# Row maxima of an attention: one standing scratch tile for their discarded scores, and another place for the scores in the second stretch

## The chip, the cores and the metric

The kernel runs on one core of a Trainium2 chip. The metric is the device time of one execution in microseconds (us); less is better. The core's engines are named as in the profile: PE multiplies matrices (PEld is its loading of weights), DVE is the vector engine, ACT the engine that evaluates functions, POOL the general one, SP an engine that here only issues DMAs. Each engine runs its own list of instructions in order and waits on semaphores that the others count up.

## The reference

Four layers act on x of 2048 rows by 640 columns, each as `x = x + layer(layernorm(x))`, in the order A, B, A, B. A is a linear attention. B has 32 heads of 20 columns and cuts the 2048 rows into four segments of 512; within a segment it is a causal softmax attention, and a memory carries what earlier segments left.

```
for s in range(N):                      # N = 4 segments of L = 512 rows
    qs, ks, vs = q[:, :, s], k[:, :, s], v[:, :, s]
    logits = jnp.einsum("bhqd,bhkd->bhqk", qs, ks) * scale + mask
    p = _softmax(logits, axis=-1)
    a_dot = jnp.einsum("bhqk,bhkd->bhqd", p, vs)
    pq = phi(qs)
    num = jnp.einsum("bhld,bhde->bhle", pq, M)
    den = jnp.einsum("bhld,bhd->bhl", pq, z)[..., None] + 1e-6
    a_mem = num / den
    o = g * a_mem + (1.0 - g) * a_dot
    outs.append(o)
    pk = phi(ks)
    M = M + jnp.einsum("bhld,bhle->bhde", pk, vs)
    z = z + jnp.einsum("bhld->bhd", pk)
```

## The kernel before

Two streams of work are written into one program. `dense` holds the layer norms, the projections, the memories and the outputs; `attend` holds the softmax of the two B layers. `run` takes a piece of the one or of the other by their costs so far, so PE's list is a hand-made mixture of both, and it stands as written (`MANUAL = ("PE",)`). The lists of DVE, ACT, POOL and SP are put in order by the framework's scheduler.

The attention goes by iterations, 8 groups of four heads for each of 4 segments and two B layers: 64 iterations in all, each of three stretches (`STRETCHES`, L54). Between two stretches PE gets a share of the dense stream. An entry of a stretch is an operation, its number, and how many groups back the group lies on which it works:

- `max` (`row_max`, L988) makes scores with queries on the partitions (L999), two banks a time, and lets DVE take each row's maximum over the masked keys (L1006). DVE's instruction must write the masked scores somewhere; nobody reads them. They go to a tile named `junk`. One `max` makes two or four such pieces: numbers 0 and 2 (with this table's numbering, `MAXES[0]` and `MAXES[2]`) two pieces of 512 columns, 1 and 3 a piece of 384 and one of 128 for each bank, 4 two of 256 for each. A piece is two DVE instructions: the reduction, and a short one that reads the accumulator out into `mg`.
- `split` (L1010) turns the maxima into two 16-bit rows `m2` on DVE (L1015, L1016); `rows` (L1019) transposes them on PE (L1024), copies them on ACT (`mt`, L1026) and sends them with two DMAs of SP's queue (L1029) into the query tile `qs` of the group.
- `exp` (`scores`, L1032) makes scores with keys on the partitions, the row maxima already taken off by the rows that `rows` has put into `qs` (L1041: two banks for each `exp`), then ACT takes the exponential (L1045) and POOL the causal mask (L1052).
- `sum` (L1060, L1068) weighs the values, `copy` (L1072) empties that bank, `out` (`normalize`, L1076) transposes back (L1081) and divides (L1084, L1091).

So in the second stretch of an iteration the new group gets its fourth maximum, and the group before it, whose rows were sent in the first stretch, its first scores.

PSUM has 8 banks, handed out in turn to both streams (`bank`, L144): the bank that PE fills now must have been read out by the engine that used it 8 banks ago. The tile `junk` comes from a pool with one buffer (`bufs=1`): each piece asks for the tile anew, and it is released when the piece before has been read out.

Of the kernel before, what the change touches and what calls it, by code (L numbers as in the profile page):

```python
# [11 lines left out]
BF16 = mybir.dt.bfloat16  # L12
# [9 lines left out]
P = 128  # L22
C = D // P
SEG = 512
# [29 lines left out]

STRETCHES = [[("exp", 4, 2), ("max", 0, 0), ("max", 1, 0), ("sum", 0, 2), ("rows", 0, 1), ("sum", 1, 2), ("sum", 3, 2),
              ("sum", 2, 2), ("copy", 0, 2), ("max", 2, 0)],
             [("out", 0, 2), ("max", 3, 0), ("exp", 0, 1), ("exp", 1, 1)],
             [("exp", 2, 1), ("exp", 3, 1), ("max", 4, 0), ("split", 0, 0), ("load", 0, 0)]]


# [70 lines left out]
class Kernel:  # L131
# [702 lines left out]
    def open_b(self):  # L834
        self.bp = self.ctx.enter_context(self.tc.tile_pool(name="attn", bufs=1))
        nc = self.nc
        self.ks = [self.bp.tile([P, 2, SEG], F16, name=f"ks{j}") for j in range(3)]
        one = self.bp.tile([P, 2, SEG], F16, tag="nat", name="one", bufs=2)
        nc.vector.memset(one[:2], M_ONE)
        for k in self.ks:  # L840
            for a in (60, 124):
                nc.sync.dma_start(k[a:a + 2], one[:2])
# [147 lines left out]
    def row_max(self, G, todo):  # L990

        nc, bp, qs, ks = self.nc, self.bp, G["qs"], G["ks"]
        bs = [self.bank() for _ in range(2)]
        cost = 0
        for p, i, a in todo:
            n = (i + 1) * P
            for par in range(2):
                r = slice(64 * par, 64 * par + 60)
                nc.tensor.matmul(bs[par][:, a:a + n], qs[r, p, i * P:(i + 1) * P], ks[r, p, :n],  # L999
                                 start=True, stop=True)  # L1000
                cost += n * COL
        for par in range(2):
            for p, i, a in todo:
                n = (i + 1) * P
                junk = bp.tile([P, SEG], BF16, tag="junk", name="junk", bufs=1)
                nc.vector.tensor_tensor_reduce(junk[:, :n], bs[par][:, a:a + n], self.maskw[:, SEG - n:],  # L1006
                                               1.0, NEG, OP.add, OP.max, G["mg"][:, par, p, i:i + 1])
        return cost

# [318 lines left out]
```

## Time and profile before

| what | us |
|---|---|
| median of 3 runs (1766.63 to 1768.07) | 1767.3 |
| span of the profiled execution, first to last instruction | 1765.2 |
| PE busy in it | 1677.6 |
| DVE busy | 1190.2 |
| ACT busy | 969.2 |
| POOL busy | 519.6 |
| PE idle in the two B layers' attention (349 to 950, and 1238 to 1733) | 24.3 and 26.4 |

The median is 2.1 us above the span of the profiled execution. Busy is the time in which an engine has an instruction in work. PE's instructions overlap, and the profile models their ends, so a wait of PE that is shorter than the end of the matmul before it is not seen as idle time. A row of the waits says who waited, for whose instruction, how long in total, how often, and the longest.

### The profile page before, as it was taken

Reading aid. Unit: us, or ns where it says so; the run is one execution under the profiler, and the core shown is the slowest. Engines: PE = TensorE matmul, PEld = TensorE weight load, DVE = VectorE, ACT = ScalarE, POOL = GpSimd, SP = SyncE. Lnnn points to the kernel's source line nnn. Section 1 sums busy time; section 2 is a strip of 40 time slices with the busy share of each in tenths; the row PEclk is TensorE's granted clock in tenths of the full one; section 3 lists DMA queues with packets and bytes.
Section 4 is the critical chain, followed back from the end, with each engine's and each line's share of the span. In section 5 each row is a group of like instructions: output and inputs, shape, how many; then the busy total and the mean of one; then the engine's idle time right before and its main releaser. Section 6 shows DMA issues by size and latency. Waiting matters only on the chain.

```text
span 1765.2 us, 36353 instructions
## 1 busy us (share of the span) xinstructions
PE 1677.6 (95%) x13032; PEld 1046.0 (59%) x13032; DVE 1190.2 (67%) x3856; ACT 969.2 (55%) x1818; POOL 519.6 (29%) x982
## 2 busy tenths in 40 slices
PE   5989999999999999999989999999999999999998
PEld 4666667564565566456556777566446545644555
DVE  8554444487787777758865466746877877878773
ACT  5454443347656645666666453333665575666664
POOL 1533441012123412333342211221422432233442
PEclk9999999999999999999999999999999999999999
DMA  7432343422322332352211303433232323323422
GB/s 247 154 133 105 142 168 110 154 71 71 109 86 67 106 99 80 115 180 77 81 42 39 113 31 120 158 113 120 67 98 84 110 80 106 96 81 106 145 95 91
DMA packets 118333, 187.61 MB, mean 106 GB/s; under 512 B 13948, under 2 KB 79612, under 8 KB 115848
## 3 DMA queue, kind: packets, MB, share of 16 engines
q1 hardware_dynamic: 105896, 142.68, 25.5%
q0 software_dynamic: 3040, 21.63, 3.4%
q10 hardware_dynamic: 9216, 20.98, 3.1%
q8 instruction: 103, 1.69, 0.4%
q14 instruction: 78, 0.64, 0.1%
HBM read 106.05 MB, written 78.64 MB: 105 GB/s over the span
## 4 chain that ended last, share of the span: by engine, by line
PE 69%; DVE 13%; ACT 7%; issue 3%; DMA 3%; POOL 3%; SPq 1%; ACTq 0%; DVEq 0%; POOLq 0%
PE ps L388 30%; PE ps L374 15%; PE ps L1068 6%; DVE junk L1006 5%; ACT pe L1045 3%; PE ps L313 3%; PE ps L1041 3%; PE ps L999 3%; PE ps L557 3%; PE ps L443 2%; DMA pqi<-pqd 1%; PE ps L1081 1%; PE ps L884 1%; PE ps L723 1%; DVE st L331 1%
## 5 line engine op out<-in xcount | busy, mean ns | idle before, releaser
L1006 DVE CUSTOM_DVE_ANT_0 junk<-ps,maskw 128x512 bf16<-128x512 f32 (+3 forms) x1024 | 499.1, 487 | 91.3 <-PE ps L999 31.7
L1045 ACT ACTIVATE pe<-ps,lsc 128x512 f32<-128x512 f32 x640 | 394.6, 696 | 105.0 <-PE ps L1041 96.1
L1052 POOL TENSOR_SCALAR_AFFINE_SELECT pe<-pe 128x256 f32<-128x256 f32 (+1 forms) x640 | 231.3, 367 | 446.6 <-ACT pe L1045 442.4
L388 PEld LDWEIGHTS <-xT 128*128 128x128 f16 x2880 | 281.0, 98 | 115.6 <-issue 10.6
L388 PEld LDWEIGHTS <-oT 128*128 128x128 f16 x1920 | 185.9, 98 | 82.5 <-issue 7.5
L1068 PE MATMUL ps<-pe,v 128*32 128x512 f32 (+3 forms) x2048 | 161.1, 436 | 9.2 <-POOL pe L1052 4.2
L388 PE MATMUL ps<-w_Bo,oT 128*128 128x320 f16 x960 | 142.4, 301 | 2.3 <-ACT oT L317 1.2
L374 PE MATMUL ps<-xT,w_Bq 128*128 128x512 f16 x600 | 140.2, 379 | 1.9 <-ACT pe L1045 0.6
L374 PE MATMUL ps<-xT,w_Bk 128*128 128x512 f16 x600 | 138.8, 379 | 1.9 <-DVE tmp L1091 1.1
L388 PE MATMUL ps<-w_Bv,xT 128*128 128x320 f16 x960 | 139.7, 299 | 0.5 <-ACT v L421 0.5
L388 PE MATMUL ps<-w_Ak,xT 128*128 128x320 f16 x960 | 137.2, 300 | 0.6 <-ACT r L402 0.5
L999 PE MATMUL ps<-ks,qs 60*128 60x512 f16 (+3 forms) x1024 | 123.4, 299 | 10.2 <-DVE mg L1006 3.6
L1041 PE MATMUL ps<-qs,ks 62*128 62x384 f16 (+3 forms) x1024 | 112.7, 298 | 8.9 <-DVE mg L1006 5.7
L849 DVE SCALAR_TENSOR_TENSOR nat<-ps,nat 128x512 f16<-128x512 f32 x80 | 54.9, 686 | 83.8 <-ACT nat L848 78.3
L414 POOL TENSOR_SCALAR e<-e 128x320 f32<-128x320 f32 (+1 forms) x52 | 82.1, 1578 | 88.5 <-ACT e L410 85.5
L1068 PEld LDWEIGHTS ps<-pe,v 128*32 128x32 f32 x2048 | 63.4, 109 | 67.6 <-issue 43.0
L374 PEld LDWEIGHTS <-w_Bk 128*128 128x128 f16 x600 | 57.3, 98 | 71.6 <-issue 10.5
L848 ACT ACTIVATE nat<-ps 128x512 f16<-128x512 f32 x80 | 48.2, 602 | 92.5 <-PE ps L374 71.7
L374 PEld LDWEIGHTS <-w_Bq 128*128 128x128 f16 x600 | 56.8, 98 | 66.9 <-issue 8.9
L421 ACT ACTIVATE v<-ps 128x320 f32<-128x320 f32 x96 | 41.8, 437 | 90.3 <-PE ps L388 89.8
L336 POOL TENSOR_TENSOR rs<-rs,mhalf 128x1 f32<-128x1 f32 x48 | 27.0, 564 | 216.6 <-DVE rs L335 203.6
L466 POOL TENSOR_TENSOR xn<-xn,xo 128x320 f32<-128x320 f32 x56 | 48.7, 871 | 136.3 <-ACT xn L465 135.6
(220 smaller groups left out, 2680.2 us busy)
## 6 DMA issues: line engine op xcount, KB each, us to landing
x<-xn ACTq DMA_DIRECT2D x48, 320.0 KB
qs<-qd SPq DMA_DIRECT2D x128, 120.0 KB
ks<-kd SPq DMA_DIRECT2D x128, 120.0 KB
xo<-x SPq DMA_DIRECT2D x48, 320.0 KB
pqi<-pqd SPq DMA_DIRECT2D x32, 320.0 KB
qd<-nat SPq DMA_DIRECT2D x40, 256.0 KB
kd<-nat SPq DMA_DIRECT2D x40, 256.0 KB
x<-in_A_x SPq DMA_DIRECT2D x16, 320.0 KB
```

The costliest lines, as they stand in the source:

```text
L313: nc.tensor.transpose(pt[:, (c - c0) * P:(c - c0 + 1) * P], src[:, c * P:(c + 1) * P], self.ident)
L374: nc.tensor.matmul(p, w[:, c, a, t * P:(t + 1) * P], xT[:, c, b, :], start=k == 0, stop=k == 3 * C - 1)
L388: nc.tensor.matmul(p, xT[:, c, a, i * P:(i + 1) * P], w[:, c, b, n * HN:(n + 1) * HN], start=k == 0, stop=k == 3 * C - 1)
L414: nc.gpsimd.tensor_scalar(e, e, 1.0, eps, op0=OP.min, op1=OP.add)
L557: nc.tensor.matmul(p, xs[:, i, a, c * P:(c + 1) * P], pk[i][:, b, cols], start=k == 0, stop=k == 3 * NT - 1)
L849: nc.vector.scalar_tensor_tensor(nat[:, 1], p, QK_SHIFT, nat[:, 0], op0=OP.mult, op1=OP.subtract)
L999: nc.tensor.matmul(bs[par][:, a:a + n], qs[r, p, i * P:(i + 1) * P], ks[r, p, :n], start=True, stop=True)
L1006: nc.vector.tensor_tensor_reduce(junk[:, :n], bs[par][:, a:a + n], self.maskw[:, SEG - n:], 1.0, NEG, OP.add, OP.max, G["mg"][:, par, p, i ...
L1041: nc.tensor.matmul(b[:, a:a + n], ks[r, p, j * P:(j + 1) * P], qs[r, p, j * P:], start=True, stop=True)
L1045: nc.scalar.activation(e, b, AF.Exp, scale=self.lsc)
L1052: nc.gpsimd.affine_select(d, d, pattern=pat, compare_op=OP.is_ge, fill=0.0, base=0, channel_multiplier=-1)
L1068: nc.tensor.matmul(G["pv"][32 * h4:32 * h4 + 32, j * P:], v[j][:, h * E1:h * E1 + 32], G.pop((p, par, j)), start=j == 0, stop=j == 2, skip ...
```

## The change

The scratch tile becomes one that stands for the whole program, made once in `open_b`, and a piece writes to the columns in which its scores stand in their bank (`a:a + n`), no longer to the first columns (`:n`) of a tile of its own. So a piece of 384 columns and one of 128 no longer write over each other, nor do the two pieces of 256 of a bank. In the second stretch the two `exp` now come ahead of `max` 3. What is computed is the same.

```diff
-             [("out", 0, 2), ("max", 3, 0), ("exp", 0, 1), ("exp", 1, 1)],
+             [("out", 0, 2), ("exp", 0, 1), ("exp", 1, 1), ("max", 3, 0)],
...
         self.ks = [self.bp.tile([P, 2, SEG], F16, name=f"ks{j}") for j in range(3)]
+        self.junk = self.bp.tile([P, SEG], BF16, name="junk")
...
                 n = (i + 1) * P
-                junk = bp.tile([P, SEG], BF16, tag="junk", name="junk", bufs=1)
-                nc.vector.tensor_tensor_reduce(junk[:, :n], bs[par][:, a:a + n], self.maskw[:, SEG - n:],
+                nc.vector.tensor_tensor_reduce(self.junk[:, a:a + n], bs[par][:, a:a + n], self.maskw[:, SEG - n:],
                                                1.0, NEG, OP.add, OP.max, G["mg"][:, par, p, i:i + 1])
```

The lines from 838 to 1004 of the kernel before stand one line later in the changed one, so L999 is L1000 there; L1006 and what follows keep their numbers.

DVE's list at the second stretch of iteration 20, before (names carry buffer numbers; the row ends with the engines on whose semaphores it waits, DVE itself among them):

```order
L1084 RECIPROCAL rc4_9227<-ps_9222 128x16 [waits PE_49]
L1091 TENSOR_TENSOR tmp_9229<-ps_9222,rc4_9227 128x320 [waits DVE_49]
L1006 ISA junk_9238,mg_9109<-ps_9232,maskw_77 128x384 [waits PE_49]
L1006 ISA mg_9109 128x1
L346 BN_STATS st_9790<-xn_9112 128x6 [waits Pool_49]
L1006 ISA junk_9240,mg_9109<-ps_9232,maskw_77 128x128 [waits DVE_49]
L1006 ISA mg_9109 128x1
L1006 ISA junk_9242,mg_9109<-ps_9233,maskw_77 128x384 [waits DVE_49,PE_49]
L1006 ISA mg_9109 128x1
L1006 ISA junk_9244,mg_9109<-ps_9233,maskw_77 128x128 [waits DVE_49]
L1006 ISA mg_9109 128x1
```

The same place in the changed kernel:

```order
L1084 RECIPROCAL rc4_8900<-ps_8895 128x16 [waits PE_49]
L1091 TENSOR_TENSOR tmp_8902<-ps_8895,rc4_8900 128x320 [waits DVE_49]
L346 BN_STATS st_9423<-xn_8793 128x6 [waits Pool_49]
L1006 ISA junk_2761,mg_8790<-ps_8925,maskw_77 128x384 [waits PE_49]
L1006 ISA mg_8790 128x1
L1006 ISA junk_2761,mg_8790<-ps_8925,maskw_77 128x128
L1006 ISA mg_8790 128x1
L1006 ISA junk_2761,mg_8790<-ps_8926,maskw_77 128x384 [waits DVE_49,PE_49]
L1006 ISA mg_8790 128x1
L1006 ISA junk_2761,mg_8790<-ps_8926,maskw_77 128x128 [waits DVE_49]
L1006 ISA mg_8790 128x1
```

The four pieces of the maximum now stand together, the other stream's L346 is ahead of them; the first piece of 128 waits for nothing, and the two waits on DVE that are left are for the piece two places back that wrote the same columns, not for the one directly ahead.

PE's list at the same stretch, before (L1081 is `out`, L999 the fourth maximum, L1041 the scores; the weights are loaded by the row above each matmul):

```order
L1081 MATMUL ps_9222<-ident_68,oTf_9194 128x128 x3
L999 LDWEIGHTS qs_9104
L999 MATMUL ps_9232<-ks2_2760,qs_9104 128x384
L999 LDWEIGHTS qs_9104
L999 MATMUL ps_9233<-ks2_2760,qs_9104 128x384 [waits DVE_49]
L999 LDWEIGHTS qs_9104
L999 MATMUL ps_9232<-ks2_2760,qs_9104 128x128
L999 LDWEIGHTS qs_9104
L999 MATMUL ps_9233<-ks2_2760,qs_9104 128x128
L1041 LDWEIGHTS ks1_2759 [waits DMAHW0_49]
L1041 MATMUL ps_9246<-qs_8877,ks1_2759 128x512 [waits DVE_49]
```

The same place in the changed kernel:

```order
L1041 MATMUL ps_8905<-qs_8574,ks1_2759 128x512 [waits DMAHW0_49]
L1041 LDWEIGHTS ks1_2759 [waits DMAHW1_49]
L1041 MATMUL ps_8910<-qs_8574,ks1_2759 128x512 [waits DVE_49]
L1041 LDWEIGHTS ks1_2759
L1041 MATMUL ps_8915<-qs_8574,ks1_2759 128x512 [waits DVE_49]
L1041 LDWEIGHTS ks1_2759
L1041 MATMUL ps_8920<-qs_8574,ks1_2759 128x512 [waits PE_49]
L1000 LDWEIGHTS qs_8785
L1000 MATMUL ps_8925<-ks2_2760,qs_8785 128x384 [waits DVE_49]
L1000 LDWEIGHTS qs_8785
L1000 MATMUL ps_8926<-ks2_2760,qs_8785 128x384 [waits DVE_49]
```

The four scores have moved ahead of the four matmuls of the maximum; the wait for the DMA of the rows (DMAHW) is met that much earlier, and the banks are handed out in the new order. Apart from such swaps PE's list is unchanged over the whole program.

## The prediction

> **What bounds the kernel now.** I read the engines' busy shares first, then the chain of work that ended last, then the busy time of the two attention parts, then PE's waits, and last the timeline of single iterations. The shares:
>
> ```profile
> PE 1677.6 (95%) x13032; PEld 1046.0 (59%) x13032; DVE 1190.2 (67%) x3856; ACT 969.2 (55%) x1818; POOL 519.6 (29%) x982
> ...
> PE 69%; DVE 13%; ACT 7%; issue 3%; DMA 3%; POOL 3%; SPq 1%; ACTq 0%; DVEq 0%; POOLq 0%
> PE ps L388 30%; PE ps L374 15%; PE ps L1068 6%; DVE junk L1006 5%; ACT pe L1045 3%; PE ps L313 3%; PE ps L1041 3%; PE ps L999 3%; PE ps L557 3%; PE ps L443 2%; DMA pqi<-pqd 1%; PE ps L1081 1%; PE ps L884 1%; PE ps L723 1%; DVE st L331 1%
> ```
>
> PE is busy for 95% of the span, so nothing is won but PE's waits. The row maxima are the largest group on the chain that is not PE's: DVE L1006 has 5% of the span, about 88 us. The change touches the attention alone; its two parts, by the busy time of stretches (us from start, length, PE, PEld, DVE, ACT, POOL):
>
> ```profile
> 349.00:950.00 601.00, 576.72 (x4764) 347.79 (x4763) 450.55 (x1623) 368.99 (x687) 178.81 (x404) 1.00 0.29 89
> 1238.00:1733.00 495.00, 468.57 (x3918) 263.74 (x3918) 380.18 (x1388) 316.69 (x580) 175.49 (x383) 1.00 0.30 96
> ```
>
> There PE is idle for 24.3 and 26.4 us: 51 us in 1096, a ceiling for what the profile shows. DVE is at 831 us, 76%: no bound by itself, but it falls behind in bursts, and then holds PE. The waits of PE (waiter, releaser, total, times, longest):
>
> ```profile
> PE ps L1041 <- DVE mg L1006: 5.7, 9, 2.7
> PE ps L1068 <- POOL pe L1052: 4.2, 8, 1.5
> PE ps L999 <- DVE mg L1006: 3.6, 6, 1.9
> ...
> PE ps L313 <- ACT pe L1045: 2.8, 6, 0.9
> PE ps L999 <- ACT pe L1045: 2.8, 9, 0.5
> PE ps L388 <- DVE xT L318: 2.7, 1, 2.7
> PE pm L1024 <- DVE m L1016: 2.2, 2, 1.2
> ...
> PE ps L999 <- DVE oT L318: 1.2, 2, 0.6
> ```
>
> They are a floor, since a wait under the modelled end of the last matmul does not show. How much is hidden at the second stretch's scores is seen from their form in the groups, from one undisturbed iteration and from one that waited:
>
> ```profile
> L1041 PE MATMUL ps<-qs,ks 62*128 62x512 f16 x256 | 46.8, 376 | 7.9 <-DVE mg L1006 5.2 <-DMA qs<-mt 0.8 <-DVE tmp L1091 0.7
> ...
> 545.40 0.39 PE L999 MATMUL ps<-ks,qs 60*128 60x384 f16 x4
> 545.63 0.60 PE L1041 MATMUL ps<-qs,ks 62*128 62x512 f16 x4
> ...
> 735.26 0.95 PE L1041 MATMUL ps<-qs,ks 62*128 62x512 f16 x4
> ```
>
> Undisturbed, four scores take 0.60 us; 64 iterations would be 38.4. The group has 46.8 busy and 7.9 idle, so PE loses 16.3 us there in all, of which 8.4 do not show as idle. These four matmuls take the banks that the maxima 0 to 2 of the first stretch filled, and start when DVE has read them out.
>
> **The change part by part.** *The scratch tile.* What a wait of DVE for its own piece costs, in iteration 20 (start, duration):
>
> ```profile
> 712.58 0.17 DVE L1016 SCALAR_TENSOR_TENSOR m<-mg,m 128x16 f16<-128x16 f32 x1
> 712.67 0.68 DVE L1006 CUSTOM_DVE_ANT_0 junk<-ps,maskw 128x512 bf16<-128x512 f32 x1
> 713.28 0.09 DVE L1006 DVE_READ_ACCUMULATOR2_ANT mg<- 128x1 f32 x1
> 713.51 0.69 DVE L1006 CUSTOM_DVE_ANT_0 junk<-ps,maskw 128x512 bf16<-128x512 f32 x1
> 714.13 0.08 DVE L1006 DVE_READ_ACCUMULATOR2_ANT mg<- 128x1 f32 x1
> 714.36 0.56 DVE L1006 CUSTOM_DVE_ANT_0 junk<-ps,maskw 128x384 bf16<-128x384 f32 x1
> 714.84 0.08 DVE L1006 DVE_READ_ACCUMULATOR2_ANT mg<- 128x1 f32 x1
> 714.96 0.29 DVE L1006 CUSTOM_DVE_ANT_0 junk<-ps,maskw 128x128 bf16<-128x128 f32 x1
> ```
>
> The first piece waits for nothing of DVE and starts 0.08 us before the instruction ahead has ended (712.75). The piece of 128 waits for the read-out directly ahead (end 714.92) and starts 0.04 after it: 0.12 us lost. A piece that waits for that and for PE as well starts 0.14 after it (713.37 to 713.51): 0.22 lost, though PE was long done. A wait for an earlier piece, one that has ended, should cost nothing. Counted in DVE's list: directly behind a read-out and waiting for it stood 291 pieces with one semaphore and 345 with two; now 0 and 187. That frees 291 x 0.12 + 158 x 0.22 = 70 us of DVE, 1.1 us in each iteration. The Trainium skill says otherwise: "VectorE: DVE Perf Modes", section "The DRAIN you can't avoid", finds a semaphore behind each of eight operations no dearer than one behind the last, and its table of rules advises fewer operations, not fewer semaphores. By that the 70 us would be none, the terms below would go, and the time would stay; the rows above, 0.08 before the end against 0.04 and 0.14 after it, speak against it.
>
> *Where DVE's time reaches PE.* Between the first piece of max 0 and the last of max 2, three of the eight pieces lose their wait (a 128, a 384 with two semaphores, a 128): 0.12 + 0.22 + 0.12 = 0.46 us earlier at the banks for which PE's four scores wait. Of their 16.3 us, 2.7 is not DVE's (below); of the other 13.6 I take 9 away, as the waits are some tenths long (0.95 against 0.60 is 0.35), but a few longer than 0.46. Bounds: nothing, and 13.6. The end of max 4, the split and the transpose L1024 behind it come up to 1.1 us earlier: of 2.2 us I take 2 (bounds 0 and 4, some being hidden). Of the 3.6 us in which a maximum's matmul waits for a maximum I take 2 (bounds 0 and 3.6).
>
> *The order in the second stretch.* Four matmuls of the maximum take 0.23 us of PE (545.40 to 545.63), and the scores pass them. The ring of banks stays as it was: the first two places go to scores instead of the maximum, and the last two, which wait for max 2, to the maximum instead of the scores, so PE stands at the same bank for about as long. ACT gets its four exponentials 0.23 us or more earlier, and the banks that it reads come free earlier: of 2.8 + 2.8 us that PE waits for exponentials I take 1 (bounds 0 and 5.6). Max 3 reaches DVE later, by the four scores (0.60 us at most), behind max 2; DVE has the division L1084, L1091 to do in that time, and its own chain is 1.1 us shorter, so I cost it at nothing; uncovered it would be up to 0.6 us in those iterations where DVE has nothing else.
>
> What the scores pass on SP's queue is nothing, but they meet the landing of the rows earlier. Iteration 20 shows the wait:
>
> ```profile
> 713.88 0.27 ACT L1026 ACTIVATE mt<-pm 32x128 f16<-32x128 f16 x1 [0.26 <-PE pm L1024]
> ...
> 714.88 1.31 SPq L1029 DMA_DIRECT2D qs<-mt  x2
> ...
> 717.86 0.39 PE L999 MATMUL ps<-ks,qs 60*128 60x384 f16 x4
> ...
> 720.91 0.34 PEld L1041 LDWEIGHTS <-ks 62*128 62x128 f16 x4 [2.93 <-DMA qs<-mt]
> ...
> PEld L1041 <- DMA qs<-mt: 5.1, 5, 2.9
> ```
>
> PE's idle 2.66 us there stand under DVE in the waits, but the weights' row names the DMA; this is the 2.7 taken off above. Such waits are seen 5 times. Each now loses the cover of 0.23 us: 1.2 us. I double it for iterations in which the rows land just in time, and where PE, waiting less, arrives sooner: 2.5. Bounds: 0, and 64 x 0.23 = 15 if it met every iteration.
>
> *DVE's other work.* The scheduler now puts the pieces of a maximum together, and dense instructions that stood between them before or behind. PE's waits for such (L318) are 2.7 and 1.2 us in the rows above. A dense read-out that is passed by two to four pieces is late by 0.6 to 1.4 us, if it was ready. I charge 2 us in all (bounds -2, since DVE as a whole is earlier, and 10, a quarter of the iterations by 0.6 us).
>
> **The sum.** -9 - 2 - 2 - 1 + 2.5 + 2 = -9.5; half a us more for short waits that no row shows makes -10. Against the profiled execution's span of 1765.2 that is 1755.2; the median lies 2.1 above the span, so 1757.3.
>
> **The rivals.** *It moves nothing that counts* (the DVE time freed is not PE's). For it: DVE is idle for 24% of the attention, and a wait of PE that ends earlier may meet the next one, ACT's or POOL's (4.2 us at L1068), just behind it. Against it: the 13.6 us at the scores, whose last releaser is the maxima's read-out. Then -9 shrinks to -3, and with 4.5 of costs the time is 1767 to 1769. By the rule of the Trainium skill above it would come out here too. Chance 0.18.
>
> *The rows land too late* (slower). Place: the first score of the second stretch. The maximum was what PE did while two DMAs of 1.31 us to issue were under way; scores now come first, and a score that waits holds the maximum behind it and so DVE too, which then starts max 3 late and hands on a later split, later rows. It decides when rows land less than 0.23 us ahead of the scores. For it: 5 seen waits, and PE arrives sooner if DVE lets it. Against it: the other 59 iterations show none. If a third of the iterations lost 0.23 for PE and 0.3 for DVE behind, 21 x 0.53 = 11 us stand against the gains of 14. To end slower, the scores' term must shrink with them, as PE's wait for DVE only becomes one for the rows: with -3 in its place the gains are 8, the costs 11 + 2, and +5 makes 1772. Chance 0.12.
>
> *More than forecast*: all 13.6 at the scores, 4, 3.6 and 5.6 go, with costs of 1: about -26, 1741. Chance 0.15.
>
> **How the numbers follow.** The forecast, some -5 to -15, has 0.55, the rivals 0.18, 0.12 and 0.15. The range leaves out 0.1 on each side: down to -21, 1746, half way into the third rival; up to 1768.5, which holds most of the first. About 0.2%, 3.5 us, is what a measurement of this kernel can tell from no change. Faster by more: 0.55 + 0.15 = 0.70; within: 0.18; slower: 0.12.
>
> **What would show it.** Right: the groups of L1006 keep their durations, yet the starts of 128-column pieces lie 0.08 before the end of the read-out ahead; the row of 62x512 scores plus its idle falls from 54.7 to about 45, with a like wait not rising at the 60x384 matmuls; PE's idle in the two parts falls from 51 towards 43. Wrong: if pieces without the wait start no earlier; if PE's wait for rows (5.1 us at PEld) doubles or triples; if PE's waits for L318 or L849 grow by more than 5 us; or if the wait reappears whole at max 3's matmuls.

## The result, and the profile after

The changed kernel takes 1758.06 us (median of 4 runs, 1756.36 to 1761.22), the kernel before 1767.68 in runs beside it (1766.63 to 1768.37): 9.6 us less, ratio 0.9948, 95% interval 0.9933 to 0.9962. The forecast was 1757.3. The profiled execution is the slowest of its four: 1761.22 us with a span of 1759.5.

The shares of the engines, and the chain of work that ended last by engine and by line, of the changed kernel:

```profile
PE 1679.1 (95%) x13032; PEld 1052.1 (60%) x13032; DVE 1160.8 (66%) x3856; ACT 971.3 (55%) x1818; POOL 516.7 (29%) x982
...
PE 78%; DVE 9%; ACT 7%; issue 2%; POOL 2%; DMA 2%; SPq 0%; ACTq 0%; DVEq 0%; POOLq 0%
PE ps L388 33%; PE ps L374 16%; PE ps L1068 7%; PE ps L1041 4%; PE ps L313 4%; PE ps L1000 3%; ACT pe L1045 3%; PE ps L557 3%; PE ps L443 3%; DVE junk L1006 2%; PE ps L1081 1%; PE ps L885 1%; PE ps L723 1%; POOL e L414 1%; PE ps L877 1%
```

DVE's part of the chain falls from 13% to 9%, that of the maxima's pieces from 5% to 2%. How the pieces follow each other in iteration 20 (start, duration):

```profile
714.61 0.56 DVE L1006 CUSTOM_DVE_ANT_0 junk<-ps,maskw 128x384 bf16<-128x384 f32 x1
715.09 0.08 DVE L1006 DVE_READ_ACCUMULATOR2_ANT mg<- 128x1 f32 x1
715.09 0.28 DVE L1006 CUSTOM_DVE_ANT_0 junk<-ps,maskw 128x128 bf16<-128x128 f32 x1
```

The piece of 128 starts with the read-out ahead (715.09, end 715.17): 0.08 before its end, where it stood 0.04 behind it. The busy time of the two attention parts (length, then PE, PEld, DVE, ACT, POOL, the granted clock, and two numbers on the DMA), and the waits of PE that the prediction spoke of:

```profile
349.00:950.00 601.00, 575.47 (x4761) 349.09 (x4760) 436.59 (x1623) 370.29 (x687) 178.21 (x404) 1.00 0.28 89
1238.00:1733.00 495.00, 475.83 (x3986) 270.17 (x3984) 364.87 (x1390) 321.80 (x589) 178.07 (x391) 0.99 0.31 98
```

```profile
PE ps L1068 <- POOL pe L1052: 7.1, 9, 1.6
PE ps L1000 <- ACT pe L1045: 4.1, 13, 0.6
PE ps L1041 <- DMA qs<-mt: 3.9, 1, 3.9
...
PE ps L1000 <- DVE mg L1006: 1.3, 5, 0.4
...
PE pm L1024 <- DVE m L1016: 1.2, 1, 1.2
...
PEld L1041 <- DMA qs<-mt: 4.8, 4, 4.0
```

PE's idle time is 25.5 and 19.2 us, 44.7 in place of 50.7, all of it won in the second part. PE's visible waits for maxima are nearly gone, at the scores (0.2 over all their forms, was 5.7) and at the maxima (1.3, was 3.6); it waits longer for exponentials, ACT's at the maxima (4.1, was 2.8) and, through POOL's masks L1052, at the sums (7.1, was 4.2). The groups of maxima and scores, where hidden waits are read, and that of the maxima's pieces with all forms in one row (count, then busy, mean ns, idle ahead of them); of these the two maxima rows and the pieces of before:

```profile
L999 PE MATMUL ps<-ks,qs 60*128 60x384 f16 x256 | 46.1, 327 | 4.0 <-DVE mg L1006 2.6 <-DVE oT L318 0.6 <-ACT pe L1045 0.5
...
L999 PE MATMUL ps<-ks,qs 60*128 60x128 f16 x256 | 30.1, 216 | 0.0
...
L1006 DVE CUSTOM_DVE_ANT_0 junk<-ps,maskw 128x512 bf16<-128x512 f32 (+3 forms) x1024 | 499.1, 487 | 91.3 <-PE ps L999 31.7 <-DVE mg L1006 0.5
```

And of the changed kernel:

```profile
L1000 PE MATMUL ps<-ks,qs 60*128 60x384 f16 x256 | 50.1, 324 | 3.7 <-ACT pe L1045 1.1 <-DVE mg L1006 0.8 <-DVE oT L318 0.6
...
L1041 PE MATMUL ps<-qs,ks 62*128 62x512 f16 x256 | 40.4, 384 | 3.9 <-DMA qs<-mt 3.9
...
L1000 PE MATMUL ps<-ks,qs 60*128 60x128 f16 x256 | 33.0, 216 | 0.0
...
L1006 DVE CUSTOM_DVE_ANT_0 junk<-ps,maskw 128x512 bf16<-128x512 f32 (+3 forms) x1024 | 459.0, 486 | 70.5 <-PE ps L1000 42.6
```

The pieces with their idle time fall from 590.4 to 529.5 us, 61 less, at the same mean duration. In that their waits for PE grow by 10.9 (31.7 to 42.6); all else falls by 72. The scores' row falls from 54.7 to 44.3, 10.4 less; but the maxima's matmuls rise from 50.1 to 53.8 and from 30.1 to 33.0, 6.6 more. So a good half of the wait at the scores has moved to the maxima behind them.

### The profile page after: what moved, and what is told of

Read it like the earlier page. It is cut to its first block, busy times and chain, and to the rows that moved or that the text cites. A ratio compares the mean times of both kernels' runs of the same rounds, so it can differ in the third digit from the quotient of the medians.

```text
span 1759.5 us, 36387 instructions
## 1 busy us (share of the span) xinstructions
PE 1679.1 (95%) x13032; PEld 1052.1 (60%) x13032; DVE 1160.8 (66%) x3856; ACT 971.3 (55%) x1818; POOL 516.7 (29%) x982
## 4 chain that ended last, share of the span: by engine, by line
PE 78%; DVE 9%; ACT 7%; issue 2%; POOL 2%; DMA 2%; SPq 0%; ACTq 0%; DVEq 0%; POOLq 0%
PE ps L388 33%; PE ps L374 16%; PE ps L1068 7%; PE ps L1041 4%; PE ps L313 4%; PE ps L1000 3%; ACT pe L1045 3%; PE ps L557 3%; PE ps L443 3%; DVE junk L1006 2%; PE ps L1081 1%; PE ps L885 1%; PE ps L723 1%; POOL e L414 1%; PE ps L877 1%
## 5 line engine op out<-in xcount | busy, mean ns | idle before, releaser
L1006 DVE CUSTOM_DVE_ANT_0 junk<-ps,maskw 128x512 bf16<-128x512 f32 (+3 forms) x1024 | 459.0, 486 | 70.5 <-PE ps L1000 42.6
L1052 POOL TENSOR_SCALAR_AFFINE_SELECT pe<-pe 128x256 f32<-128x256 f32 (+1 forms) x640 | 230.2, 366 | 462.6 <-ACT pe L1045 458.2
L1068 PE MATMUL ps<-pe,v 128*32 128x512 f32 (+3 forms) x2048 | 162.8, 439 | 13.7 <-POOL pe L1052 7.1
L1000 PE MATMUL ps<-ks,qs 60*128 60x384 f16 (+3 forms) x1024 | 127.5, 298 | 9.5 <-ACT pe L1045 4.1
L1041 PE MATMUL ps<-qs,ks 62*128 62x512 f16 (+3 forms) x1024 | 106.9, 300 | 5.7 <-DMA qs<-mt 3.9
L1068 PEld LDWEIGHTS ps<-pe,v 128*32 128x32 f32 x2048 | 65.3, 110 | 74.3 <-issue 45.8
L1000 PEld LDWEIGHTS <-qs 60*128 60x128 f16 x1024 | 50.2, 94 | 77.2 <-issue 50.6
```

The costliest lines, as they stand in the source:

```text
L1006: nc.vector.tensor_tensor_reduce(self.junk[:, a:a + n], bs[par][:, a:a + n], self.maskw[:, SEG - n:], 1.0, NEG, OP.add, OP.max, G["mg"][:, ...
L1041: nc.tensor.matmul(b[:, a:a + n], ks[r, p, j * P:(j + 1) * P], qs[r, p, j * P:], start=True, stop=True)
L1052: nc.gpsimd.affine_select(d, d, pattern=pat, compare_op=OP.is_ge, fill=0.0, base=0, channel_multiplier=-1)
L1068: nc.tensor.matmul(G["pv"][32 * h4:32 * h4 + 32, j * P:], v[j][:, h * E1:h * E1 + 32], G.pop((p, par, j)), start=j == 0, stop=j == 2, skip ...
```

## The experiments

The theory behind the forecast: the gain is DVE's, from pieces that no longer wait for the read-out ahead, and the order adds about 1 us. The first rival: the order brings it. Four kernels ran on one chip: the changed one again, each part alone, and the changed one with the old columns.

**The changed kernel again.** No edit.

> The changed kernel once more, for a second profile and a ratio on the chip of the three runs beside it. Both theories expect 0.993 to 0.996 of the time before, and in the profile a row of 62x512 scores with idle of about 44 us (44.3 in the first profile of after, 54.7 before) and 60x384 matmuls of the maxima near 53 to 54 us.

1758.32 us, ratio 0.9943 (0.9931 to 0.9956); span 1756.0. The same groups as above:

```profile
L1000 PE MATMUL ps<-ks,qs 60*128 60x384 f16 x256 | 49.7, 322 | 3.7 <-ACT pe L1045 1.3 <-DVE mg L1006 0.8 <-DVE oT L318 0.6
...
L1041 PE MATMUL ps<-qs,ks 62*128 62x512 f16 x256 | 39.3, 381 | 3.0 <-DMA qs<-mt 3.0
```

As expected, the scores' row is at 42.3 and that of the maxima at 53.4: the second profile confirms the first.

**The scratch tile alone.** The second stretch keeps the order of before.

```diff
-             [("out", 0, 2), ("exp", 0, 1), ("exp", 1, 1), ("max", 3, 0)],
+             [("out", 0, 2), ("max", 3, 0), ("exp", 0, 1), ("exp", 1, 1)],
```

> The scratch tile alone: a standing tile with own columns, the order of the second stretch as before. Theory, DVE's freed waits bring nearly all: 9 to 6 us faster than before (ratio 0.995 to 0.9965), the pieces of L1006 with their idle about 60 us less than 590.4, the row of 62x512 scores with its idle at 44 to 47 us. Rival, the order brings it: within 2 us of before (0.999 to 1.001), and the row at 50 us or more although DVE is as much freed.

1768.95 us, ratio 1.0003 (0.9994 to 1.0012): nothing. Yet its groups read as the theory wants:

```profile
L1000 PE MATMUL ps<-ks,qs 60*128 60x384 f16 x256 | 45.5, 326 | 1.4 <-DVE oT L318 0.6 <-ACT pe L1045 0.2
L1041 PE MATMUL ps<-qs,ks 62*128 62x512 f16 x256 | 43.7, 378 | 5.3 <-DMA qs<-mt 3.0 <-DVE mg L1006 1.1 <-DVE tmp L1091 0.4
...
L1006 DVE CUSTOM_DVE_ANT_0 junk<-ps,maskw 128x512 bf16<-128x512 f32 (+3 forms) x1024 | 460.7, 486 | 74.8 <-PE ps L1000 45.8 <-DVE mg L1006 0.5 <-PE ps L1068 0.3
```

DVE's pieces are 55 us shorter (535.5), the scores 5.7 (49.0), the maxima 3.2 (46.9). So DVE is freed, and PE's waits for it are shorter, and the time stands. The theory in this form is refuted, and so is its expectation of 6 to 9 us; what the first rival expected holds in the time, but not in its row of 50 us or more.

**The order alone.** Scores ahead of maximum 3, with the pool's scratch tile.

```diff
-        self.junk = self.bp.tile([P, SEG], BF16, name="junk")
...
-                nc.vector.tensor_tensor_reduce(self.junk[:, a:a + n], bs[par][:, a:a + n], self.maskw[:, SEG - n:],
+                junk = bp.tile([P, SEG], BF16, tag="junk", name="junk", bufs=1)
+                nc.vector.tensor_tensor_reduce(junk[:, :n], bs[par][:, a:a + n], self.maskw[:, SEG - n:],
```

> The order alone: scores ahead of max 3, and the pool's scratch tile as before, so that 649 pieces wait for the read-out directly ahead (636 before). Theory: within 3 us of before (0.998 to 1.002), pieces of L1006 with idle within 10 us of 590.4; the row of 62x512 scores with idle may fall by 2 to 6 us, but then the 60x384 matmuls of the maxima with idle rise by about as much, since the wait for DVE's banks only moves behind the scores. Rival: 6 to 10 us faster (0.994 to 0.9965).

1765.38 us, ratio 0.9984 (0.9975 to 0.9992): 2.3 less.

```profile
L999 PE MATMUL ps<-ks,qs 60*128 60x384 f16 x256 | 51.5, 322 | 6.2 <-DVE mg L1006 2.3 <-ACT pe L1045 1.6 <-DVE tmp L1091 0.8
...
L1041 PE MATMUL ps<-qs,ks 62*128 62x512 f16 x256 | 40.3, 381 | 3.6 <-DMA qs<-mt 3.4
...
L999 PE MATMUL ps<-ks,qs 60*128 60x128 f16 x256 | 33.5, 215 | 0.0
...
L1024 PE MATMUL pm<-ident,m 128*32 128x128 f16 x64 | 14.1, 221 | 5.5 <-DVE m L1016 5.3 <-DVE oT L318 0.2
```

The pieces stay at 591.8 us. The scores fall by 10.8 (43.9), more than expected, and the wait comes back: maxima 57.7 and 33.5 (11.0 more), and the split's transpose waits 5.3 us for DVE in place of 2.2. As expected the wait only moves, and the first rival, by which the order alone brings 6 to 10 us, fails too.

**The changed kernel with the old columns.** All pieces write the standing tile from column 0.

```diff
-                nc.vector.tensor_tensor_reduce(self.junk[:, a:a + n], bs[par][:, a:a + n], self.maskw[:, SEG - n:],
+                nc.vector.tensor_tensor_reduce(self.junk[:, :n], bs[par][:, a:a + n], self.maskw[:, SEG - n:],
```

> The changed kernel, but every piece writes the standing tile from column 0 on, as it did with the pool's tile: 649 pieces wait for the read-out directly ahead. Theory, what counts is that no piece waits for the one directly ahead: the time and the profile of the order alone, within 2 us of that run, so 0.998 to 1.002 of before; pieces of L1006 with idle within 10 us of 590. Rival, that the tile stands outside the pool is what counts: the time of the changed kernel, 0.993 to 0.996.

1765.33 us, ratio 0.9977 (0.9967 to 0.9987), that of the order alone (1765.38); that the tile stands outside the pool brings nothing. The pieces are back at 590.1:

```profile
L1006 DVE CUSTOM_DVE_ANT_0 junk<-ps,maskw 128x512 bf16<-128x512 f32 (+3 forms) x1024 | 499.3, 488 | 90.8 <-PE ps L1000 30.4 <-DVE mg L1006 0.5
```

Against the changed kernel, 1758.32 on the same chip, it differs in the columns alone, and in how the scheduler orders its lists for them: with the new order DVE's waits for its own read-outs are worth 7.0 us. With the old order they were worth nothing. The prediction weighed the Trainium skill, "VectorE: DVE Perf Modes", section "The DRAIN you can't avoid", by which more semaphores cost nothing; these 7.0 us and the 61 us of DVE speak against carrying that rule to a wait for the instruction directly ahead.

**Where the tile's time went.** The first four kernels were read once more, matmul by matmul: the time from one start to the next, less the usual one for that pair of forms (the lower quartile over the six traces), added up by the waiting form; what the trace shows under the halved clock is kept apart. These are estimates: another threshold for what counts as excess moves them by up to 3 us, differences between columns by up to 2. In us, one profiled execution each:

| excess at | before | tile alone | order alone | changed | changed, again |
|---|---|---|---|---|---|
| first four scores, L1041 of 512 columns | 30.9 | 24.4 | 19.3 | 19.4 | 17.7 |
| maxima, 384 and 128 columns | 10.8 | 7.2 | 21.5 | 16.1 | 16.6 |
| split's transpose, L1024 | 3.3 | 1.1 | 6.3 | 2.4 | 2.4 |
| sums, L1068 of 512 and 256 columns | 55.2 | 64.4 | 52.4 | 60.7 | 60.9 |
| transposes, L313 | 23.3 | 20.5 | 18.5 | 16.1 | 15.9 |
| halved clock | 4.9 | 12.6 | 9.2 | 11.5 | 9.5 |

The tile alone gains 6.5 + 3.6 + 2.2 + 2.8 = 15.1 at scores, maxima, split and transposes, and loses 9.2 at the sums and 7.7 by the clock (the profiled execution of before has a mean clock of 0.997, above the 0.994 of its 25 runs here, so the last row differs by less on average). The loss at the sums lies at the first ones, of 512 columns; the wait for the masks, at those of 256, is as before (two rows of the kernel before, two of the tile alone):

```profile
L1068 PE MATMUL ps<-pe,v 128*32 128x512 f32 x512 | 68.2, 603 | 5.0 <-ACT r L412 1.8 <-DVE m L1016 1.2 <-ACT pkt L878 0.7
L1068 PE MATMUL ps<-pe,v 128*32 128x256 f32 x512 | 46.7, 382 | 4.2 <-POOL pe L1052 4.2
...
L1068 PE MATMUL ps<-pe,v 128*32 128x512 f32 x512 | 69.1, 610 | 12.8 <-DVE xT L318 4.3 <-DVE m L1016 3.2 <-ACT r L412 2.1
L1068 PE MATMUL ps<-pe,v 128*32 128x256 f32 x512 | 48.0, 387 | 4.1 <-POOL pe L1052 4.1
```

Three of the waits at first sums, 2.1, 1.3 and 3.9 us, are late in the run; the longest, with what DVE did ahead of it:

```profile
1390.42 0.82 DVE L767 TENSOR_REDUCE rca<-pqi 128x32 f32<-128x640 f32 x1 [3.25 <-POOL pqi L764]
...
1391.16 1.48 DVE L1015 TENSOR_SCALAR m<-mg 128x16 f16<-128x16 f32 x1
...
1393.24 1.94 PE L1068 MATMUL ps<-pe,v 128*32 128x512 f32 x8 [3.87 <-DVE xT L318]
```

DVE's list has L767 of the dense work ahead of the split L1015 there, and L767 waits 3.25 us for POOL. The split is also slow there: beside POOL's L764 (1391.07 to 1394.11) its two instructions take 1.48 and 1.12 us, where the changed kernel takes 0.17 for each, ahead of L764. In the changed kernel the split stands ahead of L767 in that iteration. In the order alone it does not, and there PE waits for it at the transpose, 3.42 of the 5.3 us named above:

```profile
1385.92 0.82 DVE L767 TENSOR_REDUCE rca<-pqi 128x32 f32<-128x640 f32 x1 [2.68 <-POOL pqi L764]
1386.65 1.48 DVE L1015 TENSOR_SCALAR m<-mg 128x16 f16<-128x16 f32 x1
...
1389.68 0.29 PE L1024 MATMUL pm<-ident,m 128*32 128x128 f16 x1 [3.42 <-DVE m L1016]
```

So a second pair of theories: the tile's gain in the old order was lost to that placement, or freed DVE time does not reach PE in the old order whatever stands there. Four kernels took the wait away by another operand; what they leave out is DVE's dependence on L764, so their factors are others.

**L767 freed, four times.** Before, tile alone, order alone and changed, each with this edit:

```diff
-        nc.vector.tensor_reduce(rc, q3, axis=AX.X, op=OP.add)
+        nc.vector.tensor_reduce(rc, L["zb"][:, :D].rearrange("p (h e) -> p h e", e=DH), axis=AX.X, op=OP.add)
```

> The kernel before, but the sums of L767 read zb instead of pqi, so that DVE no longer waits there for POOL's multiplication L764 (the read-out's factors are then others; what is left out is that dependence, the work is the same). It is the base of the three runs beside it. DVE waits 5.7 us at L767 before, three times ahead of a split: 0 to 4 us faster than before (0.998 to 1.000).

> The scratch tile alone, with the sums of L767 freed in the same way. In the tile alone PE stood 7.3 us at three first sums (1249, 1325 and 1393 us), behind splits that DVE's list has behind L767, which waited for POOL. First theory, the tile's freed time was worth 5 to 6 us also in the old order and was lost at these three places: now 4 to 7 us faster than the freed kernel before, the three waits below 2 us in all. Second theory, in the old order freed DVE time does not reach PE, whatever stands at L767: within 2 us of the freed kernel before.

> The order alone, with the sums of L767 freed. Both theories: 2 to 4 us faster than the freed kernel before, as without it (ratio of the order alone 0.9984), with the maxima's 60x384 matmuls and their idle still 7 us above before (57.7 against 50.1).

> The changed kernel with the sums of L767 freed. First theory: 8 to 11 us faster than the freed kernel before, about what tile and order bring one by one (so their sum explains it within 2 us). Second theory: also 8 to 11 us faster, but then 5 us or more beyond the sum of the two.

Medians 1774.72, 1774.23, 1771.22 and 1762.17 (before, beside them, 1767.55; ratios 1.0042, 1.0039, 1.0023 and 0.9967, each within 0.0013). The base was a miss: freed, it is 7 us slower. POOL's list, in order, points to why: L770, which no longer has to wait, now stands between the masks for which the sums wait (kernel before, freed):

```profile
1394.00 3.03 POOL L764 TENSOR_TENSOR pqi<-pqi,zb 128x640 f32<-128x640 f32 x2
1396.98 1.27 POOL L770 TENSOR_TENSOR pqi<-pqi,rca 128x640 f32<-128x640 f32 x1
1398.21 0.41 POOL L1052 TENSOR_SCALAR_AFFINE_SELECT pe<-pe 128x256 f32<-128x256 f32 x1
```

PE's wait for the masks, 4.2 us before with 1.5 the longest, grows by 6.7:

```profile
PE ps L1068 <- POOL pe L1052: 10.9, 10, 3.5
```

Against this base the tile alone is 0.5 us faster, the order 3.5, both 12.6, which is 8.6 beyond their sum; in the new order the tile brings 9.1. The three waits at first sums are gone (their excess is 34.4 us, 32.9 in the freed kernel before), waits of up to 3.7 us stand at the sums of 256 columns in both, and the tile still brings nothing in the old order: the place of L767 in the list is not the cause by itself. The test is not a clean one, since from the freed kernel before to the freed tile alone PE's waits for the masks rise from 10.9 to 12.8 us and the mean clock of the runs falls from 0.9928 to 0.9906. The second theory's numbers came out, but for the 12.6 where it said 8 to 11, and it names no mechanism; the POOL rows suggest a third theory. The sums wait for a chain of their own: scores, ACT's exponentials, POOL's masks. The tile shortens DVE's chain alone; the order sends the scores, and with them this other chain, earlier.

**The masks left out.** Before, tile alone and changed, each without POOL's 640 masks:

```diff
-        nc.gpsimd.affine_select(d, d, pattern=pat, compare_op=OP.is_ge, fill=0.0, base=0,
-                                channel_multiplier=-1)
```

> The kernel before without POOL's triangle masks L1052 (640 instructions left out, so later keys are not masked away and the values differ); the sums then wait for ACT's exponentials alone. It is the base of the two runs beside it. PE waited 4.2 us for those masks, the sums' weights 21.0 us: 3 to 10 us faster than before (0.994 to 0.998).

> The scratch tile alone, in the old order, without the masks. Third theory, what the tile frees at the scores is lost again at the sums, which wait for the chain from the scores over ACT's exponentials and POOL's masks; with the masks gone that chain is shorter, and the tile alone brings 4 to 7 us against the maskless kernel before. Second theory, in the old order freed DVE time does not reach PE: within 2 us of the maskless kernel before.

> The changed kernel without the masks. Third theory: 6 to 10 us faster than the maskless kernel before, and only 1 to 4 us beyond the tile alone beside it, since the order's earlier exponentials are no longer needed. Second theory: 8 to 11 us faster, all but 2 of it beyond the tile alone.

Medians 1758.21, 1751.35 and 1744.76; ratios to before 0.9953 (0.994 to 0.9966), 0.9911 (0.9896 to 0.9926) and 0.9871 (0.9856 to 0.9886). Without the masks the tile alone brings 6.9 us in the old order, where with them it brought nothing: within the third theory's 4 to 7, and the second falls. (About 1 us of it goes with the mean clock, 0.9950 and 0.9963, by the fit in the last section.) The third theory's other numbers missed: both together were to bring 6 to 10 us, the order 1 to 4 of them, and they bring 13.5 and 6.6. So the order does more than hasten the exponentials past the masks. Nor does the run show that the masks themselves took the tile's gain: without them POOL has less to do, L767 waits 4.0 us for it in place of 7.9 in the tile alone, and the long waits at the first sums are gone (none over 1.0). That the gain is lost to waits that come from POOL's list is supported; by which of its instructions is open. Around the two iterations with POOL's dense work the busy time by stretches shows the difference (columns as above); first the tile alone, then the tile alone without masks:

```profile
1240.00:1260.00 20.00, 16.11 (x131) 9.06 (x129) 17.55 (x61) 12.14 (x23) 13.01 (x21) 0.96 0.11 30
1380.00:1400.00 20.00, 15.76 (x123) 9.04 (x124) 15.68 (x49) 9.87 (x19) 9.79 (x15) 0.83 0.48 157
```

```profile
1240.00:1260.00 20.00, 19.67 (x190) 11.00 (x185) 16.91 (x67) 11.91 (x24) 3.82 (x3) 1.00 0.19 52
1380.00:1400.00 20.00, 19.08 (x165) 11.57 (x163) 16.01 (x66) 12.13 (x23) 4.25 (x5) 1.00 0.10 27
```

With masks PE is idle for some 4 us in each and the clock is reduced; without them it is all but full, at full clock.

**Two scratch tiles.** One for each bank of a maximum, on the changed kernel, and a buffer of exponentials fewer.

```diff
-        self.junk = self.bp.tile([P, SEG], BF16, name="junk")
+        self.junk = [self.bp.tile([P, SEG], BF16, name=f"junk{j}") for j in range(2)]
...
-                nc.vector.tensor_tensor_reduce(self.junk[:, a:a + n], bs[par][:, a:a + n], self.maskw[:, SEG - n:],
+                nc.vector.tensor_tensor_reduce(self.junk[par][:, a:a + n], bs[par][:, a:a + n], self.maskw[:, SEG - n:],
...
-PE_BUFS = 10
+PE_BUFS = 9
```

> The changed kernel with two scratch tiles, one for each of a maximum's two banks, and to make room nine buffers of exponentials in place of ten. No piece waits any more for the read-out directly ahead (187 in the changed kernel); at 0.22 us for each that is 41 us of DVE less. If DVE's maxima still set PE in the new order: 3 to 5 us faster than the changed kernel (0.9915 to 0.993 of before). If exponentials and masks are what is late now: within 2 us of the changed kernel (0.993 to 0.9955), or slower, as a buffer of theirs is missing.

1802.53 us, ratio 1.0194 (1.0177 to 1.0211): by the ratios some 44 us slower than the changed kernel.

```profile
L1006 DVE CUSTOM_DVE_ANT_0 junk<-ps,maskw 128x512 bf16<-128x512 f32 (+3 forms) x1024 | 443.1, 485 | 71.3 <-PE ps L1000 70.8
...
L1068 PE MATMUL ps<-pe,v 128*32 128x256 f32 x512 | 74.8, 388 | 21.1 <-POOL pe L1052 20.7
...
L1041 PE MATMUL ps<-qs,ks 62*128 62x512 f16 x256 | 39.2, 381 | 3.0 <-DMA qs<-mt 3.0
```

The pieces lose 15 us more (514.4), nearly all of their idle time is now for PE (70.8 of 71.3), and the scores' row stays where it was (42.2). Without the waits for PE they lose 43 us, about the 41 expected. The sums of 256 columns lose it: 74.8 + 21.1 against 47.8 + 7.1 with ten buffers. ACT's exponentials now wait 31.0 us at 43 places for PE (put down to L1024), a wait that the changed kernel's rows do not have; so the missing buffer is the likely cause, though the run changes both at once. How much the second tile would bring with ten buffers is open.

## Why the prediction was right, and where it was not

The time came out (1758.06 for 1757.3), the account behind it only in part; that the two lie 0.8 us apart is luck, as the terms below show.

- *DVE's waits.* 70 us less were counted; 72 are measured, of which 11 become waits for PE. The pieces of 128 start 0.08 before the end of the read-out as foretold. Right.
- *The scores, -9.* The row fell by 10.4, to 44.3 for "about 45". But the step gave this to the scratch tile, by 0.46 us earlier at the banks. Alone the tile lowers the row by 5.7, the order alone by 10.8, of which 11.0 come back at the maxima (6.6 of 10.4 in the changed kernel). The step that failed is the one on the order: "PE stands at the same bank for about as long" is what happened, and its consequence, that the scores' row empties into that of the maxima, was not drawn; the text even asked for a like wait not to rise there. With tile and order the maxima's excess is 16 us, with the order alone 21.5: that is what the tile takes away in the new order, with 3.9 at the split's transpose.
- *Split, -2, and maxima waiting for maxima, -2.* 2.2 to 1.2 and 3.6 to 1.3, so 3.3 of the 4 in what shows as idle. With the hidden waits the maxima lose, as just said.
- *Exponentials, -1.* At L313 2.8 to 1.3, at the maxima 2.8 to 4.1: nothing in sum. Over all of PE's instructions the waits for exponentials rise, from 9.6 to 11.7.
- *Costs.* The rows' landing did not grow (PEld 5.1 to 4.8, 4 waits for 5) and PE's waits for L318 rose by 1.0 (4.9 to 5.9); the 4.5 us charged were too many.
- *What was not in the sum.* By the table the sums lose 5.5 to 5.7 us more, and the transposes L313 gain some 7. The halved clock takes 4.6 to 6.6 more in these profiles, but not on average: over the runs the mean clock is 0.9940 before and changed. The sum was right because these, the lower net gain at the banks (7 to 8 in place of 13) and the costs not paid cancel.
- *Which part.* The prediction gave -1 to the order and nearly all else to the tile. Measured: tile alone none, order alone 2.3, both 9.4 on the same chip. The rival "it moves nothing that counts" described the tile alone in its time: a wait that ends earlier meets the next one, just behind it. But it named POOL's wait of 4.2 us at L1068, which stays at 4.1; what grew are the waits at the first sums, behind DVE's L767 and its split, which wait for POOL's L764 or run beside it. That POOL's list has a part in it, the run without masks supports. Why the tile brings 7.0 us in the new order and nothing in the old, and why both together gain 6.6 beyond the tile without masks, isn't settled.
- *The rival's time.* Its 1767 to 1769 shrinks -9 to -3 and silently drops the other gains of 5 us; by the prediction's own terms it would be near 1764.

The gain also lies elsewhere than "1.1 us in each iteration" suggests. From the first sum of a part's first iteration to that of its last, the first part takes 556.3, 555.6 and 554.3 us (before, after, again), the second 488.9, 481.1 and 480.7: four fifths and more of it comes from the second.

## What to carry to other kernels

A change that frees an engine is worth what the chain behind it lets through: when PE waits for two chains in turn, look at what PE meets behind the first one's waits before booking them as gain, and try each part alone, since here neither 0 nor 2.3 us told of the 9.4 that both bring. Moving an instruction past a wait moves the wait; look for it at the instruction that now stands there. A scratch buffer whose content nobody reads still makes an engine wait for itself, and other columns cost nothing.

## What the runs showed of the hardware

PE's clock is a term of some size here. The trace shows it at 0.50 for stretches of 3.41 us: rows of 20 us at 0.91 hold one, 0.83 two. The tile alone has six such stretches more than before has in its profile, several behind PE's waits; over its 11 runs the mean clock is 0.9923, against 0.9940 (25 runs) before, 0.9940 (9) changed and 0.9951 (11) with the order alone. Fitted over these kernels and the one with the old columns, with a level for each, 0.001 of clock goes with 0.77 us (0.11 either way); at one clock the tile alone would be 1.0 us faster than before, the order 2.0, both 9.5. So the clock explains some of the tile's missing gain, not most of it. The Trainium skill, "TensorE: Matmul & The Clock Gate", section "HAM oscillation — how this bites in real kernels", blames gaps of PE over about 3.4 us; the half and the 3.41 us agree, but in the changed kernel the clock also halved behind idle times of PE of 1.2 us (at 1251 and 1394 us), and at 1115 and 1702 with none over 0.7 in the 12 us ahead, while before it stayed full behind one of 2.7 (at 718).

An instruction of the split on DVE that starts while POOL's L764 is running ends 0.03 us behind the end of L764, in all 16 cases in six traces (before, changed twice, tile alone, order alone, old columns): it takes 0.68 to 1.52 us in place of 0.17. One that starts just ahead of L764, by less than 0.1 us, is not held up.

A wait taken from DVE made the kernel 7 us slower, with PE's wait for the masks 6.7 us longer, as it let an instruction of POOL stand ahead of two masks: in a queue in order, an early start of one is a late start of what stands behind.
